# Swapping the two operands of the output products, with the result turned on VectorE

## The chip, the cores and the metric

The kernel runs on one core of a Trainium2 chip. The metric is the device time of one execution in microseconds (us). The kernel before took 787.72 us in the median of three runs (786.14 to 789.25).

Engines: TensorE (PE, its weight loads PEld) multiplies a stationary operand of up to 128x128 with a moving operand and adds into banks of PSUM; VectorE (DVE) and ScalarE (ACT) work elementwise over 128 partitions; SyncE (SP) here only issues DMAs.

## The reference

Attention over 4 batches, 8 heads, 576 positions and 64 columns a head (half the heads see a local window of 32, half see every 32nd position), then two layers on the 2304 tokens x 512 columns that come out:

```python
def _moe_ref(x, w1, w2, w3, w_out):          # d_model 512, d_ff 1024
    a = x @ w1
    b = x @ w2
    h = a * b @ w3
    return h @ w_out

def _moe2_ref(x, w_in, w_out):               # d_model 512, d_ff 2048
    h = x @ w_in
    g = h * (1.0 / (1.0 + np.exp(-1.702 * h)))
    return g @ w_out
```

All values are float32. The change concerns the last product only, g @ w_out with g of 2304x2048 and w_out of 2048x512.

## The kernel before

A float32 product is made of three products of a shorter type. Each operand is split in a high part (a ScalarE copy, line 168) and a low part (the difference, VectorE, line 174), and TensorE adds hi x lo, lo x hi and hi x hi; `ORDER` lists these pairs.

The last layer is stage 4, from 427.5 us to the end. It goes over three blocks of 768 tokens, each block in two halves of `HT` = 384 tokens, and uses a scheme with seven products instead of eight for a 2x2 split of tokens and columns. A block has two phases:

- Eight *quads* (class `Quad`). A quad makes seven products of x with w_in (`product`, line 1233, six matmuls of 128x384 each), puts gelu on them and keeps five combinations in a `part` tile. Between its products stand pieces of the second product for the quad before.
- The *sweep* (`after`): five factors of w_out times eight chunks, 40 pieces and one left over from the last quad.

A *piece* (line 1244) is one product of a chunk of g, 128 features by 384 tokens, with 256 columns of a w_out factor. Before the change g's chunk is stationary, one of its three tiles of 128 tokens at a time, and the factor's 256 columns move: 3 token tiles x 3 pairs = nine matmuls of 128x256. The sums stand in PSUM with tokens on the partitions, in two banks: `acc[0]` has token tiles 0 and 1 (512 columns), `acc[1]` has tile 2 (256). There are 56 pieces a block, 15 in quads and 41 in the sweep, 168 in all.

Each sweep piece needs a fresh split of its chunk: a `sp` tile, seven of them, high part on ScalarE, low part on VectorE.

Six results (`Out`: c11, u1, z1, c22, c21, c12) leave PSUM in a block, as copies on ScalarE or additions on VectorE into `ob` tiles (three buffers). Four of them, c11, c22, c21 and c12, are output and go out with `put`, one DMA of 384 KB on SP each; c12 of the last block goes out in two.

SP also loads the w_out factors (line 1172, from `tdram` into a ring of eight slots of two pieces each) and the split w_in chunks of the quads to come (line 1078, `fetched`, 896 KB); such a chunk is split in turn into `hl` tiles (one ScalarE operation, two on VectorE).

The order of all this is written out as a list of times: `D(t, f, ...)` puts step f at time t, with `MM` and `PC` the assumed costs of a product and a piece. The list is sorted and emitted once; each engine then takes its own instructions in that order and waits where an operand is not there.

Of the kernel before, what the change touches and what calls it, by code (L numbers as in the profile page):

```python
# [11 lines left out]
F32 = mybir.dt.float32  # L12
# [5 lines left out]
AF = mybir.ActivationFunctionType  # L18
ALU = mybir.AluOpType
PSUM = bass.MemoryType.PSUM  # L20

P = 128
B, H, S, D = 4, 8, 576, 64
# [17 lines left out]
ORDER = ((0, 1), (1, 0), (0, 0))  # L41
BT = 768
HT = BT // 2
NB = NT // BT
NU = 8
# [82 lines left out]

def wout_units(w):

    q = w.reshape(2, NU, P, 2, 256)
    return np.stack([q[0, :, :, 1], q[0, :, :, 0], q[1, :, :, 0], q[1, :, :, 1]], axis=2)


# [1 line left out]
def body(ctx: ExitStack, tc, ql, vl, qs, vs, qmask, w1, w2, w3t, wo, win, wout, out):  # L136
    nc = tc.nc

    def pool(name, bufs=1, stack=ctx, **kw):
        return stack.enter_context(tc.tile_pool(name=name, bufs=bufs, reuse_waits="tile", **kw))  # L140
# [91 lines left out]
    def turn(k):  # L232
        turns[k] = turns.get(k, 0) + 1
        return turns[k] % 2
# [6 lines left out]
    def room(what, n, w, tag, bufs):  # L241
        if what + str(n) in lent:
            return lent[what + str(n)]
        return aq.tile([P, w], F32, tag=tag, name=tag, bufs=1 if few else bufs)

    def load_qk(n):
        if n in qraw:
            return
        b, kind, c = PIECES[n]
        if kind == "l":  # L250
            t = room("q", n, NQL, "ql", 2)
            load(t, ql[b * NB3 + c], NQL)
        else:
            t = room("q", n, NQS, "qs", 2)
            load(t, qs[b * 2 + c], NQS)
        qraw[n] = t
# [199 lines left out]
    for i in (0, 2):  # L456
        t = xas.tile([P, KC * S], F32, tag="hl"[i // 2], name="lent")
# [3 lines left out]
    wide = {}  # L461
# [38 lines left out]
    acc = {}  # L500
# [17 lines left out]
    def half_step(k, i, h):  # L518
# [11 lines left out]
            x, x, 3, BODY, op0=ALU.logical_shift_left, op1=ALU.bitwise_and  # L530
# [236 lines left out]
    def back_parts(m):  # L767

        st = {}

        def load_():
            st[0] = p1.tile([P, HB], F32, tag="abf", name="abf", bufs=4)
            nc.sync.dma_start(st[0], abdram[0, m])

        def hi():
            hold[0, m] = abs_[m // 4][:, m % 4]
            split_hi(hold[0, m][:, 0], st[0])

        def lo():
            split_lo(hold[0, m][:, 1], st[0], hold[0, m][:, 0])  # L780

        return load_, hi, lo

    STEP = 1.7
    for sw in range(2):
        for g in range(MC):
# [3 lines left out]
            i = 14 + MC * sw + g  # L790
# [13 lines left out]
    for m in range(4):  # L804
        load_, hi, lo = back_parts(m)
# [322 lines left out]
    for u in range(1, NU):  # L1128
        at = -6.6 if u == 1 else 8 + UNIT * (u - 2)
# [4 lines left out]
    for n, (lo, hi, a, b, c) in enumerate(((4, 6, 32.1, 40.2, 41.6), (5, 7, 40.05, 46.9, 47.7))):  # L1134
        lo, hi = slot[lo][:, :7 * 256], slot[hi][:, :7 * 256]
# [12 lines left out]
    p2 = pool("p2", stack=right1, side="right")  # L1148
# [33 lines left out]
    def do(at, f, *args, **kw):  # L1182
        steps4.append((at, lambda: f(*args, **kw)))
# [10 lines left out]
    class Split:  # L1194

        def __init__(self, src, room=None):
            self.src, self.room = src, room
# [37 lines left out]
                    start=(first and kk == 0 and (a, c) == ORDER[0]), stop=(kk == 1 and (a, c) == ORDER[-1]), skip_group_check=True,  # L1235
                )

    def piece(acc, b, j, i, g, opens=False, ts=range(HT // P)):

        t3 = factor[b, j, i // 2]  # L1240
        for t in ts:
            to = acc[t // 2][:, t % 2 * 256:t % 2 * 256 + 256]
            for n, (a, c) in enumerate(ORDER):
                nc.tensor.matmul(  # L1244
                    to, g.t[:, a, t * P:(t + 1) * P], t3[:, i % 2, c], start=(opens and i == 0 and n == 0 and t % 2 == 0),
                    stop=(i == NU - 1 and n == 2), skip_group_check=True,
                )

    WIDE = (slice(0, 512), slice(512, 768))

    class Out:

        def room(self):
            self.t = p2.tile([P, HT // P, 256], F32, tag="ob", name="ob", bufs=3)
            self.o = self.t.rearrange("p t n -> p (t n)")

        def copy(self, acc, n):
            if n == 0:
                self.room()
            nc.scalar.activation(self.o[:, WIDE[n]], acc[n][:, :768 - 512 if n else 512], AF.Copy)  # L1260

        def add(self, acc, n, other):
            if n == 0 and other is not self:
                self.room()
            nc.vector.tensor_tensor(self.o[:, WIDE[n]], acc[n][:, :768 - 512 if n else 512], other.o[:, WIDE[n]], op=ALU.add)

        def put(self, b, right, d, lo=0, hi=HT // P):
            c0 = b * BT + right * HT
            nc.sync.dma_start(
                out[c0 + lo * P:c0 + hi * P, d * 256:d * 256 + 256].rearrange("(t p) n -> p t n", p=P), self.t[:, lo:hi]  # L1270
            )

    MM, PC = 1.05, 1.07
    QUAD = 7 * MM + 2 * PC
    SWEEP = ((S2, 1), (S1, 4), (S3, 3), (S4, 0), (B22, 2))
    BLOCK = NU * QUAD + PC * (2 + 5 * NU)

    class Quad:

        def __init__(self, b, i, X, Y, pre):  # L1280
# [29 lines left out]
            if pre:  # L1310
                D(4.2, piece, X, b, B11, i - 1, pre.c11, True)
            D(5.27, prod, "x", 4, 5, False, False)
            D(6.32, prod, "z", 6, 2, False)
            if pre:
                D(7.37, piece, Y, b, B21, i - 1, pre.a12, True)
# [3 lines left out]
            if i == NU - 1:  # L1319
                D(8.4, piece, X, b, B11, i, self.c11, True)  # L1320
                end += PC
# [40 lines left out]
    def after(b, q, X, Y):  # L1362
        A0 = b * BLOCK + NU * QUAD + PC
        D = lambda t, *a, **k: do(A0 + t, *a, **k)
        order = [(n, i) for n in range(5) for i in range(NU)]
        pos = [s if s < 2 else s + 1 for s in range(len(order))]
        final = b + 1 == NB
        sp = [
            Split(lambda n=n, i=i: parts[i][:, SWEEP[n][1]], yq[:, i // 2, i % 2] if final and n == 4 else None) for n, i in order
        ]  # L1370
        D(PC * 2, piece, Y, b, B21, NU - 1, q.a12, True)
        for s, (n, i) in enumerate(order):
            if final and n == 4:
                for m, ts in enumerate(((0, 1), (2,))):
                    D(PC * (33 + (0, 8 * 2 / 3)[m] + i * (2 - m) / 3) + 0.01, piece, X, b, SWEEP[n][0], i, sp[s], False, ts)
            else:
                D(PC * pos[s] + 0.01, piece, (X, Y)[n % 2], b, SWEEP[n][0], i, sp[s], n == 1)
            if i % 2:
                D(PC * (pos[s] + 1) + 0.02, t_more)
            if s < 3:  # L1380
                D(-QUAD - PC + 5.3 + 0.05 * s, sp[s].hi)
                D(-QUAD - PC + (7.0, 8.3, 8.4)[s], sp[s].lo)
            else:
                ahead = 6 if final and n == 4 else 3
                D(PC * (pos[s] - ahead) + 0.1 + 0.01 * (ahead > 3), sp[s].hi)
                D(PC * (pos[s] - ahead) + 0.65 + 0.01 * (ahead > 3), sp[s].lo)
        D(PC * 3 + 0.02, t_more, 2)
        c11, u1, z1, c22, c21, c12 = (Out() for _ in range(6))
        for n in range(2):
            D(-MM + 0.05 + 0.05 * n, c11.copy, X, n)  # L1390
            D(3.3 + 1.1 * n, c11.add, Y, n, c11)
            D(PC * 9 + 0.05 + 0.02 * n, u1.copy, X, n)
            D(PC * 17 + 0.05 + 0.02 * n, z1.copy, Y, n)
            D(PC * 25 + 0.1 + 1.07 * n, c22.add, X, n, z1)
            D(PC * 33 + 0.1 + 1.07 * n, c21.add, Y, n, u1)
            D(PC * (41 - (8 / 3 if final and n == 0 else 0)) + 0.02 + 0.01 * n, c12.copy, X, n)
        D(5.6, c11.put, b, 0, 0)
        D(PC * 25 + 2.4, c22.put, b, 1, 1)
        D(PC * 33 + 2.4, c21.put, b, 1, 0)
        if final:  # L1400
            D(PC * 41 - 2.5, c12.put, b, 0, 1, 0, 2)
            D(PC * 41 + 0.1, c12.put, b, 0, 1, 2, 3)
        else:
            D(PC * 41 + 0.1, c12.put, b, 0, 1)
        if b + 1 < NB:
            n = (b + 1) * NU
            do(A0 + 2.7, W[n].hi)
            D(5.3, W[n].lo, 0, 1024)
            D(7.0, W[n].lo, 1024, 7 * 256)
            D(-NU * QUAD + 4.5 * QUAD, y_fetch, b + 1, 0)  # L1410
            D(-PC - QUAD + 0.4, y_fetch, b + 1, 1)
            for kk, at in ((0, 8.0), (1, 17.5)):
                gaps = (0.3, 1.9, 3.0, 3.7, 4.6, 4.8, 5.8, 6.0, 7.5)
                for m, g in enumerate(gaps):
                    D(at + g, lambda m=m, kk=kk, b=b: more_steps(b, kk)[m]())
            D(27.5, W[n + 1].fetch)
            D(28.5, W[n + 2].fetch)
            D(35.0, W[n + 1].hi)
            D(38.0, W[n + 1].lo, 0, 1024)
            D(39.1, W[n + 1].lo, 1024, 7 * 256)  # L1420
# [3 lines left out]
    def more_steps(b, kk):  # L1424
        if (b, kk) not in cache:
            cache[b, kk] = y_steps(kk, dict(more))
        return cache[b, kk]
# [19 lines left out]
    for b in range(NB):  # L1447
        X, Y = [None] * 2, [None] * 2
# [6 lines left out]
        q = None  # L1455
        for i in range(NU):
            q = Quad(b, i, X, Y, q)
            n = b * NU + i
            at = b * BLOCK + i * QUAD
# [42 lines left out]
```

## Time and profile before

| | us |
|---|---|
| median of three runs | 787.72 |
| the profiled execution | 789.37 |
| its span, first to last instruction | 787.6 |
| TensorE busy | 768.0 |
| VectorE busy | 543.9 |
| ScalarE busy | 469.1 |
| matmuls of the pieces (x1440 and x72) | 179.5 and 8.8 |

Busy time of matmuls overlaps, since they are pipelined: 1440 of them count 282 ns each, while one starts about 120 ns after the other. What TensorE's work costs in time is read from the chain of waits, where a run of matmuls has a length and a count. The granted TensorE clock is 0.996 over the span.

### The profile page before, as it was taken

What the parts mean: (1) busy time and instruction counts of PE and PEld (TensorE: products, weight loads), DVE (VectorE), ACT (ScalarE), POOL (GpSimd) and SP (SyncE); (2) the same over time, 40 slices, a digit from 0 to 9 for tenths busy, and PEclk for the clock granted to TensorE, in tenths of its full rate; (3) what the DMA queues carried; (4) which work ended last, traced back from release to release, by engine and by line L of the source; (5) the groups of instructions that cost most, each with busy time, mean ns of one, the idle gap of its engine ahead of it and who ended that gap; (6) DMA issues with size and microseconds to landing.
All of it is one profiled execution on the core that took longest, in us unless ns stands there. A gap on an engine that the chain in (4) does not pass through costs nothing.

```text
span 787.6 us, 17841 instructions
## 1 busy us (share of the span) xinstructions
PE 768.0 (98%) x7259; PEld 746.4 (95%) x7259; DVE 543.9 (69%) x1044; ACT 469.1 (60%) x951; POOL 7.3 (1%) x15
## 2 busy tenths in 40 slices
PE   4899999999999999999999999999999999999998
PEld 4799999988889999999999999999999999999998
DVE  4799755588458475788775788794677794677743
ACT  5777654567466273655465766674666673666552
POOL 2000000000000000000000000000000000000000
PEclk9899999999999999999999999999999999999999
DMA  8987455632887646395998738789354489343382
GB/s 262 302 306 243 134 201 201 220 113 84 267 263 257 230 145 212 138 280 209 242 288 242 312 134 255 292 279 378 112 195 150 165 274 380 109 166 104 114 280 89
DMA packets 68641, 169.82 MB, mean 216 GB/s; under 512 B 5968, under 2 KB 39248, under 8 KB 66000
## 3 DMA queue, kind: packets, MB, share of 16 engines
q1 hardware_dynamic: 68416, 168.65, 63.8%
q8 instruction: 57, 0.93, 0.5%
q14 instruction: 24, 0.20, 0.1%
q10 hardware_dynamic: 144, 0.04, 0.0%
HBM read 132.49 MB, written 36.18 MB: 214 GB/s over the span
## 4 chain that ended last, share of the span: by engine, by line
PE 85%; DMA 7%; DVE 4%; ACT 2%; issue 1%; SPq 0%; DVEq 0%; ACTq 0%
PE acc L1244 23%; PE ps L1233 22%; PE ps L442 22%; PE ps L909 8%; PE acc L1090 3%; PE acc L755 3%; DMA raw<-in_w 2%; DMA ql<-in_ql 2%; PE pvq L395 1%; PE sc L304 1%; DMA lent<-in_qs 1%; DMA vst<-in_vs 1%; DVE w L174 1%; ACT w L168 1%; DMA abf<-abdram 1%
## 5 line engine op out<-in xcount | busy, mean ns | idle before, releaser
L1244 PE MATMUL acc<-w,sp 128*128 128x256 f32 x1440 | 179.5, 282 | 0.0
L1244 PEld LDWEIGHTS acc<-w,sp 128*128 128x128 f32 x1440 | 177.8, 191 | 0.0
L1233 PE MATMUL ps<-yq,hl 128*128 128x384 f32 x924 | 168.1, 335 | 0.0
L1233 PEld LDWEIGHTS ps<-yq,hl 128*128 128x128 f32 x924 | 158.7, 188 | 0.9 <-DVE part L1189 0.6
L174 DVE TENSOR_TENSOR sp<-part,sp 128x384 fp32r<-128x384 f32 x136 | 71.5, 553 | 60.2 <-ACT sp L168 60.2
L442 PE MATMUL ps<-xbh,w 128*128 128x288 f32 x512 | 102.6, 295 | 0.3 <-DVE w L174 0.2
L442 PE MATMUL ps<-xah,w 128*128 128x288 f32 x512 | 102.1, 294 | 0.0
L909 PE MATMUL ps<-ab,w 128*128 128x288 f32 x576 | 81.3, 298 | 1.4 <-ACT ysb L917 1.4
L442 PEld LDWEIGHTS ps<-xbh,w 128*128 128x128 f32 x512 | 81.9, 188 | 0.8 <-DVE w L174 0.7
L442 PEld LDWEIGHTS ps<-xah,w 128*128 128x128 f32 x512 | 82.0, 188 | 0.0
L909 PEld LDWEIGHTS ps<-ab,w 128*128 128x128 f32 x576 | 77.2, 188 | 3.0 <-ACT ysb L917 1.9
L442 PE MATMUL ps<-xbl,w 128*128 128x288 f32 x256 | 77.1, 301 | 0.0
L442 PE MATMUL ps<-xal,w 128*128 128x288 f32 x256 | 76.3, 298 | 0.0
L1186 ACT ACTIVATE part<-part 128x384 f32<-128x384 f32 x72 | 37.9, 526 | 61.6 <-DVE part L1189 61.6
L168 ACT ACTIVATE sp<-part 128x384 fp32r<-128x384 f32 x136 | 64.0, 518 | 11.1 <-PE acc L1244 10.2
L442 PEld LDWEIGHTS ps<-xbl,w 128*128 128x128 f32 x256 | 48.0, 188 | 0.8
L442 PEld LDWEIGHTS ps<-xal,w 128*128 128x128 f32 x256 | 48.0, 188 | 0.4
L174 DVE TENSOR_TENSOR ab<-abf,ab 128x288 fp32r<-128x288 f32 x64 | 28.4, 454 | 26.2 <-ACT ab L168 26.2
L755 PE MATMUL acc<-w,w 128*128 128x512 f32 x192 | 44.2, 391 | 0.1
L755 PEld LDWEIGHTS acc<-w,w 128*128 128x128 f32 x192 | 35.8, 188 | 8.2 <-DVE w L174 0.5
L174 DVE TENSOR_TENSOR hl<-fetched,hl 128x1024 fp32r<-128x1024 f32 (+1 forms) x40 | 43.3, 1083 | 0.0
L168 ACT ACTIVATE ab<-abf 128x288 fp32r<-128x288 f32 x64 | 27.2, 441 | 24.7 <-DVE abf L973 21.7
(193 smaller groups left out, 1048.8 us busy)
## 6 DMA issues: line engine op xcount, KB each, us to landing
w<-tdram SPq DMA_DIRECT2D x84, 512.0 KB, 4.7
fetched<-widram SPq DMA_DIRECT2D x20, 896.0 KB, 6.8
raw<-in_win SPq DMA_DIRECT2D x8, 1024.0 KB, 6.2
widram<-x SPq DMA_DIRECT2D x8, 896.0 KB, 7.1
raw<-in_wout SPq DMA_DIRECT2D x7, 1024.0 KB, 7.2
tdram<-raw SPq DMA_DIRECT2D x6, 896.0 KB, 5.8
tdram<-sums SPq DMA_DIRECT2D x6, 896.0 KB, 9.1
raw<-in_w3t SPq DMA_DIRECT2D x10, 512.0 KB, 4.9
```

Of the source, the lines that this page charges most:

```text
L168: nc.scalar.activation(hi, src, AF.Copy)
L174: e.tensor_tensor(lo, src, r(hi), op=ALU.subtract)
L304: nc.tensor.matmul(sc[32 * h:32 * h + 32, u, NJ * r:NJ * r + NJ], t[rows, at_:at_ + 32], t[rows, QW + QPAD + at_:QW + QPAD + at_ + NJ], st ...
L395: nc.tensor.matmul(pv[rows, h // 2, :, i], v[:, i, h], ps[:, i, h], start=True, stop=True)
L442: nc.tensor.matmul(ps, ws[a][m // 2][:, at:at + P], xh[c][:, k, cols], start=(k == 0 and (a, c) == ORDER[0]), stop=(k == KC - 1 and (a, c) ...
L755: nc.tensor.matmul(acc[f], hl[:, a, f * P:(f + 1) * P], wor[c][g], start=(g == 0 and (a, c) == ORDER[0]), stop=(g == MC - 1 and (a, c) == ...
L909: nc.tensor.matmul(yacc[n], wfs[a][k][:, n * P:(n + 1) * P], hold[s % 2, k][:, c], start=(k == 0 and (a, c) == ORDER[0]), stop=(k == MC - ...
L1090: nc.tensor.matmul(st[0], wfs[a][k][:, n * P:(n + 1) * P], hold[hb, k][:, c], start=(k == 0 and (a, c) == ORDER[0]), stop=(k == MC - 1 and ...
L1186: nc.scalar.activation(out(), src(), func)
L1233: nc.tensor.matmul(ps, w[a][:, f * 256 + kk * P:f * 256 + (kk + 1) * P], yq[:, b, kk, c], start=(first and kk == 0 and (a, c) == ORDER[0]) ...
L1244: nc.tensor.matmul(to, g.t[:, a, t * P:(t + 1) * P], t3[:, i % 2, c], start=(opens and i == 0 and n == 0 and t % 2 == 0), stop=(i == NU - ...
```

## The change

The two operands exchange sides. A w_out factor's 128 columns become the stationary operand and g's 384 tokens move: 2 column halves x 3 pairs = six matmuls of 128x384 a piece. The sums stand transposed in PSUM: output columns on the partitions, tokens along the bank, `acc[n]` with 384 tokens of column half n.

To store rows of tokens again, VectorE turns the result in blocks of 32x32 (`turn`, from an `ob` tile into an `ot` tile of 192 tokens; `turn_one` for the last output, straight from PSUM). A block of 32 columns and 32 tokens is turned within its 32 partitions, so the columns that end up side by side come from four groups of 32 partitions: `wout_units` reorders w_out's columns so that each group holds 64 neighbouring output columns. `put` writes one group per DMA, four for each `ot` tile. In all 26 transposes are added, and 13 stores become 104. `ob` has two buffers instead of three and `ot` three. `PC` goes from 1.07 to 1.04. In the last block the last eight pieces go by column halves instead of token tiles.

```diff
 def wout_units(w):
-    q = w.reshape(2, NU, P, 2, 256)
+    q = w.reshape(2, NU, P, 2, 4, 2, 32).transpose(0, 1, 2, 3, 5, 4, 6).reshape(2, NU, P, 2, 256)
...
-    def piece(acc, b, j, i, g, opens=False, ts=range(HT // P)):
+    def piece(acc, b, j, i, g, opens=False, ns=range(2)):
         t3 = factor[b, j, i // 2]
-        for t in ts:
-            to = acc[t // 2][:, t % 2 * 256:t % 2 * 256 + 256]
-            for n, (a, c) in enumerate(ORDER):
+        for n in ns:
+            for m, (a, c) in enumerate(ORDER):
                 nc.tensor.matmul(
-                    to, g.t[:, a, t * P:(t + 1) * P], t3[:, i % 2, c], start=(opens and i == 0 and n == 0 and t % 2 == 0),
-                    stop=(i == NU - 1 and n == 2), skip_group_check=True,
+                    acc[n][:, :HT], t3[:, i % 2, c, n * P:(n + 1) * P], g.t[:, a], start=(opens and i == 0 and m == 0),
+                    stop=(i == NU - 1 and m == 2), skip_group_check=True,
                 )
...
+        def turn(self, h):
+            self.T[h] = p2.tile([P, TB, 2, 32], F32, tag="ot", name="ot", bufs=3)
+            nc.vector.transpose(
+                self.T[h].rearrange("p b n i -> p n b i"),
+                self.t[:, :, h * 32 * TB:(h + 1) * 32 * TB].rearrange("p n (b i) -> p n b i", i=32),
             )
+        def turn_one(self, acc, n, h):
+            if h == 0:
+                self.T[n] = p2.tile([P, 2, TB, 32], F32, tag="ot", name="ot", bufs=3)
+            nc.vector.transpose(
+                self.T[n][:, h], acc[n][:, h * 32 * TB:(h + 1) * 32 * TB].rearrange("p (b i) -> p b i", i=32)
+            )
+        def put(self, b, right, d, h, n=None):
+            t, lo, wide = (self.T[h].rearrange("p b n i -> p b (n i)"), 0, 64) if n is None else (self.T[n][:, h], 32 * n, 32)
+            c0 = b * BT + right * HT + h * 32 * TB
+            to = out[c0:c0 + 32 * TB, d * 256:d * 256 + 256].rearrange("(b j) (a x) -> a j b x", j=32, a=4)
+            for a in range(4):
+                nc.sync.dma_start(to[a, :, :, lo:lo + wide], t[32 * a:32 * a + 32])
-    MM, PC = 1.05, 1.07
+    MM, PC = 1.05, 1.04
...
+                D(PC * 41 + 1.2 + 0.7 * n, c12.turn, n)
+                D(PC * 41 + 1.9 + 0.7 * n, c12.put, b, 0, 1, n)
+        for h in range(2):
+            for o, at, to in ((c11, 5.2, (0, 0)), (c22, PC * 25 + 2.3, (1, 1)), (c21, PC * 33 + 2.3, (1, 0))):
+                D(at + 0.7 * h, o.turn, h)
+                D(at + 0.7 * h + 0.7, o.put, b, *to, h)
```

The order of instructions, first VectorE's at the end of the first block, before the change. `sp` and `hl` are the low parts of the chunks, `ob<-acc,ob` the second addition of c21, and the last row is the first addition of the next block. What stands in brackets are the counters that a row waits for; DMAHW0 to DMAHW7 count landings of DMAs that SP issued.

```order
L1265 TENSOR_TENSOR ob<-acc,ob 128x256 [waits PE_49]
L174 TENSOR_TENSOR sp<-part_5831,sp 128x384 [waits Activation_49]
L174 TENSOR_TENSOR hl<-fetched,hl 128x1024 [waits DMAHW0_49]
L174 TENSOR_TENSOR sp<-part_5832,sp 128x384 [waits Activation_49]
L174 TENSOR_TENSOR hl<-fetched,hl 128x768
L174 TENSOR_TENSOR sp<-part_5833,sp 128x384 [waits Activation_49]
L174 TENSOR_TENSOR sp<-part_5834,sp 128x384 [waits Activation_49]
L1189 TENSOR_TENSOR part_5654<-ps,s_7004 128x384 [waits PE_49,Activation_49]
```

The same place after the change: two turns of c21 and two of c12.

```order
L1265 TENSOR_TENSOR ob<-acc,ob 128x384 [waits PE_49]
L174 TENSOR_TENSOR sp<-part_5825,sp 128x384 [waits Activation_49]
L1269 STREAM_TRANSPOSE ot<-ob 128x2x6x32 [waits DMAHW3_49,DMAHW2_49,DMAHW4_49,DMAHW1_49,DVE_49]
L174 TENSOR_TENSOR sp<-part_5826,sp 128x384 [waits Activation_49]
L1269 STREAM_TRANSPOSE ot<-ob 128x2x6x32 [waits DMAHW4_49,DMAHW5_49,DMAHW3_49,DMAHW2_49]
L174 TENSOR_TENSOR hl<-fetched,hl 128x1024 [waits DMAHW7_49]
L174 TENSOR_TENSOR sp<-part_5827,sp 128x384 [waits Activation_49]
L174 TENSOR_TENSOR hl<-fetched,hl 128x768
L174 TENSOR_TENSOR sp<-part_5828,sp 128x384 [waits Activation_49]
L1269 STREAM_TRANSPOSE ot<-ob 128x2x6x32 [waits DMAHW6_49,DMAHW1_49,DMAHW7_49,DMAHW0_49,Activation_49]
L1269 STREAM_TRANSPOSE ot<-ob 128x2x6x32 [waits DMAHW6_49,DMAHW1_49,DMAHW7_49,DMAHW0_49,DVE_49]
L1189 TENSOR_TENSOR part_5654<-ps,s_6866 128x384 [waits PE_49,Activation_49]
```

Each turn has a place of its own between two low parts, and waits for the landing of the four stores that read its `ot` buffer last.

SP's queue in the same sweep, from the two fetches on, before the change:

```order
L1078 DMA fetched<-widram 128x1792 [waits DMAHW0_49,DVE_49,Activation_49]
L1078 DMA fetched<-widram 128x1792 [waits DMAHW1_49,DVE_49,Activation_49]
L1172 DMA w_1624<-tdram 128x1024 [waits DMAHW2_49,PE_49]
L1269 DMA out<-ob 128x3x256 [waits DMAHW3_49,DVE_49]
L1172 DMA w_1624<-tdram 128x1024 [waits DMAHW4_49,PE_49]
L1172 DMA w_1625<-tdram 128x1024 [waits DMAHW5_49,PE_49]
```

And after it, where c22's store has become eight:

```order
L1078 DMA fetched<-widram 128x1792 [waits DMAHW7_49,DVE_49]
L1172 DMA w_1624<-tdram 128x1024 [waits DMAHW0_49,PE_49]
L1078 DMA fetched<-widram 128x1792 [waits DMAHW1_49,DVE_49,Activation_49]
L1286 DMA out<-ot 32x6x64 [waits DMAHW2_49,DVE_49]
L1286 DMA out<-ot 32x6x64 [waits DMAHW3_49]
L1286 DMA out<-ot 32x6x64 [waits DMAHW4_49]
L1286 DMA out<-ot 32x6x64 [waits DMAHW5_49]
L1286 DMA out<-ot 32x6x64 [waits DMAHW6_49,DVE_49]
L1286 DMA out<-ot 32x6x64 [waits DMAHW7_49]
L1286 DMA out<-ot 32x6x64 [waits DMAHW0_49]
L1286 DMA out<-ot 32x6x64 [waits DMAHW1_49]
L1172 DMA w_1624<-tdram 128x1024 [waits DMAHW2_49,PE_49]
```

The counters go round by eights, one step for each DMA.

## Rows read from the trace of the kernel before

**Rows 1.** The page: engine shares (busy us, share, instructions) and the chain that ended last.

```profile
PE 768.0 (98%) x7259; PEld 746.4 (95%) x7259; DVE 543.9 (69%) x1044; ACT 469.1 (60%) x951; POOL 7.3 (1%) x15
...
PE 85%; DMA 7%; DVE 4%; ACT 2%; issue 1%; SPq 0%; DVEq 0%; ACTq 0%
```

**Rows 2.** Chain of waits in order of time: start us, length us, what.

```profile
502.37 44.27 PE acc L1244 x369
```

**Rows 3.** Chain of waits, 477 to 483 us.

```profile
477.17 1.07 PE acc L1244 x9
478.24 2.08 PE ps L1233 x12
```

**Rows 4.** Groups by line and shape, VectorE: busy us, mean ns | idle before.

```profile
L174 DVE TENSOR_TENSOR sp<-part,sp 128x384 fp32r<-128x384 f32 x136 | 71.5, 553 | 60.2 <-ACT sp L168 60.2
...
L1189 DVE TENSOR_TENSOR part<-part 128x768 f32<-128x768 f32 x24 | 22.9, 953 | 1.8 <-ACT part L1186 1.8
...
L529 DVE TENSOR_SCALAR xw<-xw 128x512 int32<-128x512 int32 x20 | 8.4, 422 | 3.4 <-ACT xw L527 3.4
```

**Rows 5.** Timeline of the end: start us, length us, engine, instruction [idle before].

```profile
782.78 1.60 PE L1244 MATMUL acc<-w,yq 128*128 128x256 f32 x12
...
784.41 0.38 ACT L1260 ACTIVATE ob<-acc 128x256 f32<-128x256 f32 x1 [2.28 <-PE acc L1244]
784.82 0.34 SPq L1269 DMA_DIRECT2D out<-ob  x1
```

**Rows 6.** The tile `ob`: the stores (issue in ns, min/median/max) and their landing.

```profile
L1269 SPq DMA_DIRECT2D out<-ob x13: 344/389/1422, 508.2 to 784.8; - x13
...
DMA to landing us min/median/max: 1.7/6.2/10.9
```

**Rows 7.** Timeline of SP, 175 to 182 us.

```profile
177.43 1.85 SPq L773 DMA_DIRECT2D abf<-abdram  x4
```

**Rows 8.** Timeline of SP, 527 to 552 us.

```profile
529.82 1.22 SPq L1078 DMA_DIRECT2D fetched<-widram  x2
531.55 0.32 SPq L1172 DMA_DIRECT2D w<-tdram  x1
531.96 1.42 SPq L1269 DMA_DIRECT2D out<-ob  x1
533.71 6.80 SPq L1172 DMA_DIRECT2D w<-tdram  x4
540.60 0.39 SPq L1269 DMA_DIRECT2D out<-ob  x1
542.35 4.64 SPq L1172 DMA_DIRECT2D w<-tdram  x3
547.22 0.55 SPq L1269 DMA_DIRECT2D out<-ob  x1
```

**Rows 9.** Windows: length; PE, PEld, DVE, ACT, POOL busy; clock, DMA share, GB/s.

```profile
530.00:548.00 18.00, 18.00 (x148) 18.00 (x147) 9.78 (x19) 7.03 (x13) 0.00 (x0) 1.00 0.98 360
785.60:786.20 0.60, 0.00 (x0) 0.00 (x0) 0.00 (x0) 0.00 (x0) 0.00 (x0) 1.00 0.65 219
```

**Rows 10.** Timeline of ScalarE, 536 to 553 us.

```profile
537.51 1.70 ACT L168 ACTIVATE hl<-fetched 128x1792 fp32r<-128x1792 f32 x1 [3.27 <-DMA fetched<-widram]
...
549.42 0.53 ACT L1186 ACTIVATE part<-part 128x384 f32<-128x384 f32 x1 [1.21 <-DVE part L1189]
549.85 0.47 ACT L1298 ACTIVATE u<-ps 128x384 f32<-128x384 f32 x1
```

**Rows 11.** Waits of SP's queue: what for, us in total, times, longest.

```profile
SPq L1172 <- PE acc L1244: 172.6, 68, 14.4
```

**Rows 12.** Timeline of VectorE, 536 to 553 us.

```profile
548.83 0.56 DVE L1189 TENSOR_TENSOR part<-ps,s 128x384 f32<-128x384 f32 x1 [4.41 <-PE ps L1233]
```

**Rows 13.** Chain of waits, 544 to 560 us.

```profile
546.64 11.70 PE ps L1233 x66
```

More of the change, by code (lines that the diff above doesn't have):

```diff
@@ L1247, in piece, with __init__ @@
                 )
-    WIDE = (slice(0, 512), slice(512, 768))
+    TB = HT // 64
     class Out:
-        def room(self):
-            self.t = p2.tile([P, HT // P, 256], F32, tag="ob", name="ob", bufs=3)
-            self.o = self.t.rearrange("p t n -> p (t n)")
+        def __init__(self):
+            self.T = {}
         def copy(self, acc, n):
             if n == 0:
-                self.room()
-            nc.scalar.activation(self.o[:, WIDE[n]], acc[n][:, :768 - 512 if n else 512], AF.Copy)
+                self.t = p2.tile([P, 2, HT], F32, tag="ob", name="ob", bufs=2)
+            nc.scalar.activation(self.t[:, n], acc[n][:, :HT], AF.Copy)
@@ L1262, in add @@
         def add(self, acc, n, other):
[L1263 to L1270, printed above, removed]
-            )
@@ L1273, in body @@
-    MM, PC = 1.05, 1.07
+            self.t = other.t
+            nc.vector.tensor_tensor(self.t[:, n], acc[n][:, :HT], other.t[:, n], op=ALU.add)
+        def turn(self, h):
[3 more added lines that the diff above has]
+                self.t[:, :, h * 32 * TB:(h + 1) * 32 * TB].rearrange("p n (b i) -> p n b i", i=32),
+            )
+        def turn_one(self, acc, n, h):
[4 more added lines that the diff above has]
+            )
@@ L1373, in after @@
             if final and n == 4:
-                for m, ts in enumerate(((0, 1), (2,))):
-                    D(PC * (33 + (0, 8 * 2 / 3)[m] + i * (2 - m) / 3) + 0.01, piece, X, b, SWEEP[n][0], i, sp[s], False, ts)
+                for m in range(2):
+                    D(PC * (33 + 4 * m + i / 2) + 0.01, piece, X, b, SWEEP[n][0], i, sp[s], False, (m,))
             else:
@@ L1395, in after @@
             D(PC * 33 + 0.1 + 1.07 * n, c21.add, Y, n, u1)
[L1396 to L1404, printed above, removed]
+            if final:
+                for h in range(2):
+                    D(PC * (37 + 4 * n) + 0.1 + 0.1 * h, c12.turn_one, X, n, h)
+                    D(PC * (37 + 4 * n) + 0.11 + 0.1 * h, c12.put, b, 0, 1, h, n)
+            else:
+                D(PC * 41 + 0.02 + 0.01 * n, c12.copy, X, n)
+                D(PC * 41 + 1.2 + 0.7 * n, c12.turn, n)
+                D(PC * 41 + 1.9 + 0.7 * n, c12.put, b, 0, 1, n)
+        for h in range(2):
+            for o, at, to in ((c11, 5.2, (0, 0)), (c22, PC * 25 + 2.3, (1, 1)), (c21, PC * 33 + 2.3, (1, 0))):
+                D(at + 0.7 * h, o.turn, h)
+                D(at + 0.7 * h + 0.7, o.put, b, *to, h)
         if b + 1 < NB:
```

## The prediction

> **What bounds the kernel now.** I read the page's shares first: TensorE is busy 98% of the span, VectorE 69%, and 85% of the chain that ended last is TensorE's [rows 1]. Then the chain of waits in order of time, over the last 360 us, the stage that the change touches: it consists of TensorE pieces that join end to end. Each block's sweep is one unbroken run of 369 matmuls of 256 columns in 44.27 us, 120.0 ns each [rows 2]. Between the quads the same matmul takes 1.07/9 = 118.9 ns, and one of 384 columns 2.08/12 = 173.3 ns [rows 3]. So a column costs 0.465 ns in a short matmul and 0.451 ns in a long one, and work on the other engines is free as long as it comes before TensorE asks for its result. Last, the timelines of the queues and of VectorE where a block ends, and the end of the kernel: only there does TensorE lean on something else.
>
> **TensorE.** There are 168 pieces, 123 in sweeps and 45 between quads. A piece goes from nine matmuls of 256 columns to six of 384, which is the same number of columns. In a sweep that is 1.080 - 6 x 0.1733 = 1.040, so 0.040 us less; elsewhere 1.070 - 1.040 = 0.030. Sum: 123 x 0.040 + 45 x 0.030 = 6.3 us. If the sweep keeps half of what its matmuls take above those between quads, (1.080 - 1.070) x 123 / 2 = 0.6 us comes off; I take 6.2, bounds 5.6 to 6.3. All of it is on the path.
>
> The Trainium skill (TensorE: Matmul & The Clock Gate, section Back-to-back issue gap) gives an isolated gap of N / 2.4 + 2.5 ns for N columns. By that, an estimate, nine at 109.2 against six at 162.5 ns save 1.3 us in all. Rows 3 show 118.9 and 173.3 instead, and the sum goes by them.
>
> **VectorE.** 26 transposes are new, 22 of 384 elements a partition and four of 192. No transpose is in the trace. The nearest groups are a two-operand operation of 128x384 at 553 ns, below it one of 128x512 with a single operand at 422, above it one of 128x768 at 953 [rows 4]. I take 0.55 and 0.35 us: 22 x 0.55 + 4 x 0.35 = 13.5 us, in a stretch of 360 us in which VectorE has room. The output copies and additions keep their size (2 x 384 for 512 + 256). Beside TensorE this costs nothing, unless a transpose stands in front of something that is late already. There are two such places.
>
> **The end of the kernel.** Now the last matmul ends at 784.38, a ScalarE copy of 0.38 us follows, and one store is issued at 784.82 [rows 5]. It lands 1.7 us later, the shortest of the 13 [rows 6], and the span ends at 787.6. Afterwards each output is eight DMAs on SP, the last one sixteen. An issue there takes 344 ns at least and 389 in the median [rows 6], and four in a row go at 1.85/4 = 0.46 us [rows 7]; I take 0.42. Call the end of the last matmul T. The eight stores of c21 can start when its second addition and first turn are done, about T - 6.2. Sixteen issues (c21, and c12's first half) then last until T + 0.5, and the last eight until T + 3.9. The last lands at T + 3.9 - 0.4 + 1.7 = T + 5.2, where it is now T + 2.2. So the end gives back 3.0 us; with 0.344 us an issue it is 2.3, at most (0.46) 4.5.
>
> **Where a block ends** (547 and 666 us). Every DMA on SP carries a wait for one of eight landing counters in turn, so it waits until the eighth DMA before it has landed. Before, 13 DMAs between 529.8 and 547.2 are two fetches, three stores and eight loads [rows 8], and the queues are 98% busy there [rows 9]. The first fetch lands just before 537.5, when ScalarE takes it [rows 10], 7.7 us after its issue, and the second should by that land near 540. Afterwards the eight stores of c22 stand behind these fetches: the last two must wait for their landings. The factor loads behind them come up to 7 us later. That costs nothing, since SP has waited for TensorE to free their slots (172.6 us over the span) [rows 11], and each is used at least 14 pieces later. But the stores of c21, behind four of those loads, go out at about 540 + 0.4 + 4 x 0.4 = 542 at the earliest and 543.3 by the landings that the loads wait for; I take 543.
>
> That matters because `ot` has three buffers. c12's second turn needs the buffer of c21's first half, thus the landing of its four stores: 543 + 6.2 (median) = 549.2. Behind that turn, on VectorE, stands the addition with which the next block opens. It began at 548.83 after idling 4.41 us for TensorE [rows 12]; then ScalarE's gelu and the copy of u, from 549.42 to 550.32 [rows 10]. TensorE's fifth product adds to the bank that this copy reads, and is due at 546.64 + 4 x 1.04 = 550.8 [rows 13]. So there is 0.5 us of slack now and no waiting. After the change the sweep's end comes 41 x 0.04 = 1.65 earlier, and c21's stores 30 x 0.04 = 1.2 earlier. The copy then ends at 548.0 + 0.55 + 0.56 + 0.53 + 0.47 = 550.1, against a due time of 549.15: about 1.0 us lost. The landing that the turn waits for is the lever. With 1.7 us (the shortest) nothing is lost, with 10.9 (the longest) [rows 6] 5.7. As the packets also get smaller I take 1.2 us, twice: 2.4.
>
> **Packets.** A store of 384 KB goes from rows of 1024 bytes to 1536 rows of 256, the last output's to 128. In the last store 128 packets of 1024 bytes kept 16 engines 65% busy for 0.6 us [rows 9], 49 ns each. If a packet's price goes with its bytes, nothing is added; if every packet costs 49 ns, a store costs 1536 x 49 / 16 = 4.7 us of all engines instead of 1.2. I take some 20 ns, between them: 1.9 us a store, hidden except in the landing times above. The Trainium skill (DMA: Bandwidth & Descriptors, section Specifications) asks for at least 512 bytes for full rate and says that below this the engine reads, modifies and writes. All new stores are below; no row of before shows such a store of this size, and the rule would push towards the dear end, the second rival.
>
> **Sum:** -6.2 + 3.0 + 2.4 = -0.8 us. The profiled run took 789.4 (its span of 787.6 and 1.8 around it), which makes 788.6 on its own scale; the median of the three runs stands 1.7 below it, at 787.7, and I forecast 787.0 against that. Own range: with end 2.3 and block ends 0.8 each it is 785.4; with 5.6 saved, 4.5 and 2 x 2 it is 790.6.
>
> **Rivals.**
> Nothing is lost at the block ends. SP's stores land before VectorE gets to the last turn, as half of the 13 landings took less than 6.2 us, down to 1.7. Then -6.2 + 3.0 = -3.2: 784.5. Against it stands the 98% of the queues in just that stretch.
>
> Slower: dear small packets. c21's first four stores land 10.9 us after their issue rather than 6.2, since the stores of c22 ahead of them and their own take up to 3.5 us more each of saturated queues. That gives 1.2 + 4.7 = 5.9 us at each block end, and the end at its upper bound: -6.2 + 11.8 + 4.5 = +10.1, 797.8; halfway, 793. It decides as soon as these stores take 2.4 us longer than the median, from 8.6 us on: 2 x 3.6 + 3.0 - 6.2 = +4. For it: the largest of the present landings is from a full queue. Against: the stores carry as many bytes as before, and the stretch before and behind is at a lower load (98% is that of 18 us).
>
> The gain is not there: what six matmuls cost is set by the new roles of the operands (weights now come from the ring of factors), or 1.3 us is all. Then -1.3 + 3.0 + 2.4 = +4.1: 791.8. Against: the products at 173.3 ns are of just this form, 128x384 moving with a fresh load for each.
>
> **Chances.** Forecast 0.49, nothing lost at block ends 0.23, dear packets 0.24, no gain 0.04. A measurement of this kernel tells a change from none at about 0.5%, 3.9 us: below 783.8 is faster, above 791.7 slower. A third of the first rival and a little of the forecast lie below: 0.14. Slower: most of dear packets, half of no gain, and a tail of the forecast's block ends: 0.29. The rest, 0.57. The range for 8 in 10 reaches from 783.3 (block ends free, so -6.3 + 2.3 = -4.0, and half a per mille for the measurement) to 796 (most of the way to dear packets); the forecast's own is 785.4 to 790.6.
>
> **What will show it.** The chain's sweep pieces at 41 x 1.04 = 42.6 us, and the matmul groups with 1008 matmuls of 128x384 at L1243. The transposes near 0.55 us. SP issuing stores without a pause at the end, and some 5 us between the last matmul and the last landing. At each block end an idle time of VectorE before a transpose, released by a DMA from `ot`, and TensorE idle for 1 to 2 us about four products later. Wrong if TensorE waits inside a sweep (a turn ahead of a late split), if SP's loads of factors come too late for it, or if a store lands after more than 8.6 us.

## The result and the profile after

The changed kernel takes 793.85 us in the median of 8 runs (791.12 to 796.95), the kernel before 787.67 in 8 (786.14 to 791.42). The ratio is 1.0064, 95% interval 1.0045 to 1.0082: slower by some 5 us by the ratio and 6 by the medians. Timed a second time it was 794.74 against 788.14, ratio 1.0079 (1.0052 to 1.0106). The forecast of 787.0, a hair faster, was wrong, though 793.85 lies in its range, near its slow end.

The profiled execution took 791.34 us, near the fastest of the eight. It has a span of 789.5 us, only 1.9 over that of before. It entered the last stage 1.7 us earlier, though, at 425.68 where before began at 427.35; the stages ahead are the same code in both and move by this much from one execution to the next (this stage starts between 424.1 and 427.4 in the traces of all the runs here). From there to the end it is 363.9 us against 360.2, and so 3.6 longer.

First the page of the kernel after, its engine shares:

```profile
PE 763.1 (97%) x6755; PEld 740.8 (94%) x6755; DVE 554.8 (70%) x1070; ACT 469.1 (59%) x949; POOL 7.4 (1%) x15
```

Against [rows 1] TensorE has 4.9 us less to do and VectorE 10.9 more. Next the chain of waits of the last stage, in order of time (start us, length us, what):

```profile
500.22 28.09 PE acc L1243 x162
528.34 0.42 ACT sp L168
528.75 9.17 DMA fetched<-widram
537.94 1.69 DMA out<-ot
...
541.84 5.45 DMA out<-ot
547.52 0.44 issue
547.97 0.53 DVE part L1189
548.52 0.52 ACT part L1186
549.04 0.39 ACT u L1313
549.48 9.14 PE ps L1233 x42
...
662.42 5.00 DMA out<-ot
...
669.55 7.55 PE ps L1233 x42
...
739.51 42.66 PE acc L1243 x246
```

The last line answers to [rows 2]: the sweep of the last block takes 42.66 us where it took 44.27, just what six matmuls for nine should bring. But where [rows 13] had products joining on without a break, the chain now leaves TensorE. It runs through the landing of a store from `ot`, the turn (under "issue"), VectorE's addition, gelu, the copy of u, and only then back. The waits in that stretch, 540 to 552 us (who waited, for whom, us in total, times, longest):

```profile
DVE ot L1269 <- DMA out<-ot: 2.9, 1, 2.9
...
PE ps L1233 <- ACT u L1313: 1.9, 1, 1.9
...
PEld acc L1243 <- DVE sp L174: 0.6, 2, 0.3
```

And VectorE's timeline at the end of the first block (start us, length us, instruction, idle before and what ended it):

```profile
538.75 0.58 DVE L1269 STREAM_TRANSPOSE ot<-ob 128x384 f32<-128x384 f32 x1 [0.64 <-DMA out<-ot]
539.25 1.18 DVE L174 TENSOR_TENSOR hl<-fetched,hl 128x1024 fp32r<-128x1024 f32 x1
540.36 0.55 DVE L174 TENSOR_TENSOR sp<-part,sp 128x384 fp32r<-128x384 f32 x1
...
544.00 0.58 DVE L1269 STREAM_TRANSPOSE ot<-ob 128x384 f32<-128x384 f32 x1 [1.76 <-ACT ob L1261]
547.47 0.58 DVE L1269 STREAM_TRANSPOSE ot<-ob 128x384 f32<-128x384 f32 x1 [2.89 <-DMA out<-ot]
547.97 0.52 DVE L1189 TENSOR_TENSOR part<-ps,s 128x384 f32<-128x384 f32 x1
```

The turn at 547.47 waits for the stores of c21's first half, and right behind it stands the addition that [rows 12] shows at 548.83 with nothing to wait for but TensorE. The turn at 538.75 waits too, for stores of c22; the two rows behind it are late for that, and the `sp` split at 540.36 comes too late for the sweep (the 0.6 us of weight loads above).

The second block end has a like idle time, 1.7 us at 669. One thing differs: behind the first, 42 products take 9.14 us, behind the second 7.55. The windows show why (length; PE, PEld, DVE, ACT, POOL busy; granted clock; DMA share; GB/s):

```profile
547.50:549.50 2.00, 0.12 (x2) 0.03 (x1) 0.99 (x2) 0.98 (x3) 0.00 (x0) 1.00 0.53 102
549.50:551.50 2.00, 2.00 (x7) 2.00 (x8) 0.56 (x1) 0.71 (x2) 0.00 (x0) 0.55 1.00 379
551.50:553.50 2.00, 2.00 (x9) 2.00 (x8) 0.63 (x2) 0.52 (x1) 0.00 (x0) 0.59 0.99 305
553.50:558.00 4.50, 4.50 (x28) 4.50 (x27) 3.50 (x6) 2.21 (x5) 0.00 (x0) 1.00 0.78 190
```

Column seven: after the idle time TensorE ran at 0.55 and 0.59 in the mean of these windows, that is mostly at 1.2 GHz instead of 2.4, and took 7 and 9 matmuls in 2 us where 11 or 12 fit. That is another 1.6 us lost.

Last the end, from the timeline of all engines and the tile `ot`:

```profile
767.50 20.08 SPq L1286 DMA_DIRECT2D out<-ot  x32
...
773.66 8.48 PE L1243 MATMUL acc<-yq,w 128*128 128x384 f32 x48
...
782.19 0.65 DVE L1277 STREAM_TRANSPOSE ot<-acc 128x192 f32<-128x192 f32 x2 [3.52 <-PE acc L1243]
```

```profile
L1286 SPq DMA_DIRECT2D out<-ot x104: 315/439/1955, 506.2 to 787.1; - x104
L1269 DVE STREAM_TRANSPOSE ot<-ob x22: 535/573/586, 505.6 to 775.7; 128x384 f32<-128x384 f32 x22
L1277 DVE STREAM_TRANSPOSE ot<-acc x4: 340/362/383, 778.0 to 782.5; 128x192 f32<-128x192 f32 x4
...
DMA to landing us min/median/max: 1.5/3.5/8.1
```

The last matmul ends at 782.14, the last store is issued at 787.1, 5.0 later, and the span ends 7.4 behind the matmul; in [rows 5] these were 0.4 and 3.2.

### The profile page after: what moved, and what is told of

It is laid out like the page before. It is cut to its first block, busy times and chain, and to the rows that moved or that the text cites. A ratio compares the mean times of both kernels' runs of the same rounds, so it can differ in the third digit from the quotient of the medians.

```text
span 789.5 us, 16971 instructions
## 1 busy us (share of the span) xinstructions
PE 763.1 (97%) x6755; PEld 740.8 (94%) x6755; DVE 554.8 (70%) x1070; ACT 469.1 (59%) x949; POOL 7.4 (1%) x15
## 4 chain that ended last, share of the span: by engine, by line
PE 84%; DMA 6%; DVE 3%; ACT 3%; issue 2%; SPq 1%; DVEq 0%; ACTq 0%
PE ps L442 26%; PE ps L1233 21%; PE acc L1243 18%; PE ps L909 8%; PE acc L1090 3%; PE acc L755 3%; DMA out<-ot 2%; DMA fetched<-widram 1%; PE sc L304 1%; PE pvq L395 1%; DMA lent<-in_qs 1%; PE sc L294 1%; DMA abf<-abdram 1%; SPq L1286 1%; DMA lent<-in_ql 1%
## 5 line engine op out<-in xcount | busy, mean ns | idle before, releaser
L1243 PE MATMUL acc<-sp,w 128*128 128x384 f32 x960 | 174.2, 334 | 0.0
L1243 PEld LDWEIGHTS acc<-sp,w 128*128 128x128 f32 x960 | 167.0, 188 | 0.6 <-DVE sp L174 0.6
L1233 PEld LDWEIGHTS ps<-yq,hl 128*128 128x128 f32 x924 | 162.2, 189 | 4.6 <-ACT u L1313 4.3
```

Source lines behind the costliest of these rows:

```text
L1233: nc.tensor.matmul(ps, w[a][:, f * 256 + kk * P:f * 256 + (kk + 1) * P], yq[:, b, kk, c], start=(first and kk == 0 and (a, c) == ORDER[0]) ...
L1243: nc.tensor.matmul(acc[n][:, :HT], t3[:, i % 2, c, n * P:(n + 1) * P], g.t[:, a], start=(opens and i == 0 and m == 0), stop=(i == NU - 1 a ...
```

## The experiments

Theory: the price is three waits of known place: VectorE's turns for `ot` buffers at the block ends (with the clock behind them), the same within the sweeps, and SP's issuing at the end. Rival: stores in small rows are dear by themselves, wherever they are. Each experiment was timed beside the kernel before; us are medians.

**The changed kernel again**, for the spread of its waits. No edit.

> The changed kernel once more, beside the others of this call. The theory: VectorE's last turn at a block end waits for the landing of the stores that still read its buffer, so TensorE idles about 2 us at 543 to 550 and at 663 to 670; and where the granted clock falls after such an idle time, as it did behind the first (0.55 to 0.59 for some 4 us, 320 ns a matmul in place of 173), 1.7 us more go. So both idle times are there again, at 1.5 to 2.5 us, and behind them the clock may fall at none, one or both. Time 793 to 795, some 6 above the kernel before. The rival, that small stores are dear all over the stage: the idle times would differ from one execution to the next with the DMA load, and the products between blocks would start late in other places too.

Measured 794.74. Idle times again, 5.2 us in both together and 2.7 in the longer, and the clock down behind the first only: 42 products in 9.12 and in 7.55 us. Within the sweeps the late splits cost more than the first time (1.4 us of weight loads waiting for `sp`, four times). The last stage takes 366.1 us in this trace, 5.9 more than before, where the first profile had 3.6 more.

**c21's first turn into another buffer.** The tile `a12` is idle in a sweep and has the same size.

```diff
-        def turn(self, h):
-            self.T[h] = p2.tile([P, TB, 2, 32], F32, tag="ot", name="ot", bufs=3)
+        def turn(self, h, lent=False):
+            if lent:
+                self.T[h] = f32("a12").rearrange("p (b n i) -> p b n i", n=2, i=32)
+            else:
+                self.T[h] = p2.tile([P, TB, 2, 32], F32, tag="ot", name="ot", bufs=3)
...
-                D(at + 0.7 * h, o.turn, h)
+                D(at + 0.7 * h, o.turn, h, o is c21 and h == 0)
```

> The turn of c21's first half goes into the tile of a12, which is idle in a sweep, in place of the ring of three; all else stays, the 104 stores, their order and their size too. So c12's second turn no longer needs c21's landing. Theory: the two idle times at the block ends go (2.05 and 1.88 us), and with them the clock's fall (1.7 us where it came): 4 to 7 us less than the changed kernel, about 787 to 789. The end still costs 4 us more than before. Rival (small stores are dear, SP is held up): c12's turns or the next factors wait for something else in the same place, and the time stays within 1.5 us of the changed kernel, 792 to 795.

Measured 786.06 against 788.14, ratio 0.9979 (0.9967 to 0.9992): one buffer turns the change from slower to slightly faster, by 8.7 us in the medians against the changed kernel timed with it, 7.9 by the ratios (4.7 between the nearest ends of their intervals). That is more than the 4 to 7 expected, though not clear of it. In the trace the waits within the sweeps went too, which the 4 to 7 did not count: c21's second turn no longer needs c22's landing. Its chain of waits has no DMA from the first sweep to the last:

```profile
499.85 42.64 PE acc L1243 x246
542.49 11.71 PE ps L1233 x66
...
616.61 42.64 PE acc L1243 x246
659.25 11.69 PE ps L1233 x66
...
733.33 42.66 PE acc L1243 x246
```

SP's queue was held up as in the changed kernel, and TensorE never waited for it (its timeline: start us, length us, what):

```profile
529.60 8.56 SPq L1289 DMA_DIRECT2D out<-ot  x8
538.25 1.82 SPq L1172 DMA_DIRECT2D w<-tdram  x4
540.16 1.97 SPq L1289 DMA_DIRECT2D out<-a  x4
542.23 4.49 SPq L1289 DMA_DIRECT2D out<-ot  x4
```

Stores, rows and queues are the same as in the changed kernel; so small stores are not dear by themselves, wherever they are. Whether it is their small rows that make them land late, as the prediction's "dear packets" has it, this run cannot tell; the small stores in the kernel before, below, can. The end costs what it did (the span ends 7.5 us behind the last matmul), and with that the sum closes: -6.2 + 4.3 = -1.9, where the last stage takes 358.2 us in the trace against 360.2 before.

**Two buffers in place of three**, the suspected wait made longer: `bufs=3` of both `ot` tiles becomes `bufs=2`.

> The changed kernel with two ot buffers in place of three, nothing else: the suspected wait made longer. Theory: c12's first turn now needs c21's first half landed, and the second turn its second half, which landed 1.5 us later; so TensorE's idle time at both block ends grows from 1.9 to 3.0 us as seen so far to 3.4 to 4.5. If an idle time of that length brings the granted clock down, it now falls behind the second as it did behind the first, for 3 to 4 us (1.7 us lost each). 797 to 799. Rival (the stores themselves are the price, buffers don't matter): 793 to 795, as with three.

Measured 797.91, ratio 1.0120 (1.0078 to 1.0163). The time is as expected, but the interval overlaps that of three buffers (1.0052 to 1.0106), so it is the trace that shows the difference. The idle times are not as expected: 3.1 and 2.4 us, hardly more than with three. What grew is the wait within the sweeps, as c21's turns now both wait for c22's stores. These are TensorE's waits over the stage; the second row, its weight loads waiting for `sp`, stood at 0.6 to 1.9 in the three profiles with three buffers:

```profile
PE ps L1233 <- ACT u L1313: 5.5, 2, 3.1
PEld acc L1243 <- DVE sp L174: 4.2, 6, 1.1
```

The clock fell behind both idle times here, the second, shorter one included (TensorE's timeline: start us, length us, what, idle before):

```profile
673.25 9.12 PE L1233 MATMUL ps<-yq,hl 128*128 128x384 f32 x42 [2.37 <-ACT u L1313]
```

**The changed kernel a third time**, one run.

> The changed kernel once more, for its profile: idle times of 1.9 to 3.0 us at 548 and 669, the clock down behind the first (as in both profiles so far) and not behind the second. Should it be down behind the second and not the first, it is chance which of them it meets.

791.79 us. Idle 2.7 and 2.5 us, and no fall at all: 42 products in 7.55 and 7.58. So it isn't the place.

```profile
549.84 7.55 PE L1233 MATMUL ps<-yq,hl 128*128 128x384 f32 x42 [2.75 <-ACT u L1313]
```

**The pieces without the turns**, with `ob` back at three buffers. It leaves out the turns and so stores the output in another order.

```diff
-                self.t = p2.tile([P, 2, HT], F32, tag="ob", name="ob", bufs=2)
+                self.t = p2.tile([P, 2, HT], F32, tag="ob", name="ob", bufs=3)
...
+            nc.sync.dma_start(
+                out[c0:c0 + HT, d * 256 + lo:d * 256 + lo + wide].rearrange("(t p) x -> p t x", p=P),
+                t.rearrange("p (t x) -> p t x", t=3),
             )
...
-            for a in range(4):
-                nc.sync.dma_start(to[a, :, :, lo:lo + wide], t[32 * a:32 * a + 32])
```

> The pieces as in the changed kernel, but nothing is turned: the transposed sums go out as they lie in ob (three buffers), one store of 384 KB in rows of 1024 bytes for each output, the last in two of rows of 512; so the output is in another order than the reference's. It measures what the six matmuls of 384 columns save by themselves. Theory: sweeps of 42.6 us and no idle time at the block ends; 6.2 us less than the kernel before, 781 to 782.5. Rival (the gain is not there, or is lost within the sweeps): 785 to 788.

Measured 781.61, ratio 0.9919 (0.9900 to 0.9937): 6.5 us less, as much as the matmuls were to save. Its sweeps are 42.64, 42.64 and 42.66 us.

**Small stores alone**, in the kernel before.

```diff
-            nc.sync.dma_start(
-                out[c0 + lo * P:c0 + hi * P, d * 256:d * 256 + 256].rearrange("(t p) n -> p t n", p=P), self.t[:, lo:hi]
-            )
+            for a in range(4):
+                nc.sync.dma_start(
+                    out[c0 + lo * P:c0 + hi * P, d * 256 + a * 64:d * 256 + a * 64 + 64].rearrange("(t p) n -> p t n", p=P),
+                    self.t[:, lo:hi, a * 64:a * 64 + 64],
+                )
```

> The kernel before with its old pieces and no turn, but each store split in four of 64 columns, so rows of 256 bytes in place of 1024 and 52 stores in place of 13. Theory (the bytes set the queues' time, and SP only matters at the end): no idle time at the block ends; at the end c12's first part is out of the way, and the last four stores issue from 0.43 to 1.9 us behind the last matmul, so the last landing is 1.4 us later than now: 788.9 to 789.5. Rival (small rows are dear): TensorE waits at block ends for ob buffers or late factors, 791 or more, and a single store of 32 KB takes over 3 us to land at the end, where the queues are empty.

Measured 789.68 against 787.83, ratio 1.0017 (1.0001 to 1.0033), within the theory's 788.9 to 789.5 by the ratio (789.2). No block end shows an idle TensorE, and the stores land in 1.5 us at best, 5.2 in the median, where 384 KB in one took 1.7 and 6.2 [rows 6]:

```profile
DMA to landing us min/median/max: 1.5/5.2/9.9
```

What it lost is at its end: the span ends 4.7 us behind the last matmul (781.84), where it was 3.2. Small rows are not free, though. Behind other transfers, a store of 384 KB in rows of 1024 bytes lands 1.0 us after the transfer ahead of it in the kernel before (median); here the four parts land 0.33 us one after another, 1.3 in all, and in the changed kernel the eight parts 0.17, 1.4 in all. That is far from the 3.5 us more that "dear packets" needs.

**The end on two queues**, for the last block's c21 and c12.

```diff
-                nc.sync.dma_start(to[a, :, :, lo:lo + wide], t[32 * a:32 * a + 32])
+                queue = nc.scalar if b + 1 == NB and d != right and a % 2 else nc.sync
+                queue.dma_start(to[a, :, :, lo:lo + wide], t[32 * a:32 * a + 32])
```

> In the last block, half of the stores of c21 and c12 are issued by ScalarE, which is idle there, and half by SP. Theory: the end is bound by issuing (24 issues at 0.48 us behind one another on SP), so the last landing comes about 3 us nearer to the last matmul (from 6.6 us behind it to about 3.7), and the time is 3 us under the changed kernel, about 791. Rival (the landing of stores with rows of 128 and 256 bytes bounds the end): the last landing stays 6 us or more behind the last matmul, the time the same as the changed kernel.

Measured 791.99, 2.7 less than the changed kernel timed with it; but the ratio, 1.0052 (1.0034 to 1.0070), overlaps that one's (1.0052 to 1.0106), and the way differs from the forecast. In its profile the span ends 5.9 us behind the last matmul (785.54), where it was 7.4; by the forecast it would be 4.5 (the landing at 3.7, and the 0.8 from there to the span's end). The queues ran side by side only in part:

```profile
779.21 8.59 ACTq L1287 DMA_DIRECT2D out<-ot  x12
780.87 8.54 SPq L1287 DMA_DIRECT2D out<-ot  x13
```

SP's part began only at 780.87, 1.7 us after ScalarE's, which is what a store takes to land there. After that both issue, with pauses of up to 1.4 us on SP and 2.2 on ScalarE, and the 25 issues of the two rows take 10.2 us where 24 on SP alone took 11.8. In the order of instructions both queues draw on the same eight landing counters, and SP's last store of c22 waits for one that a store of ScalarE has to raise first. The end gave 1.5 us of the 3 forecast. What else there is in the 2.7 is not separable from the block ends, which vary from run to run, so this run bears out issuing as the bound only in part.

**A shorter end**, on top of the lent buffer: c12's column halves are turned into one tile, so that the last output needs 8 stores and not 16.

```diff
-            if h == 0:
-                self.T[n] = p2.tile([P, 2, TB, 32], F32, tag="ot", name="ot", bufs=3)
+            if n == 0:
+                self.T[h] = p2.tile([P, TB, 2, 32], F32, tag="ot", name="ot", bufs=3)
             nc.vector.transpose(
-                self.T[n][:, h], acc[n][:, h * 32 * TB:(h + 1) * 32 * TB].rearrange("p (b i) -> p b i", i=32)
+                self.T[h][:, :, n], acc[n][:, h * 32 * TB:(h + 1) * 32 * TB].rearrange("p (b i) -> p b i", i=32)
...
-                    D(PC * (37 + 4 * n) + 0.11 + 0.1 * h, c12.put, b, 0, 1, h, n)
+                    if n:
+                        D(PC * 41 + 0.11 + 0.1 * h, c12.put, b, 0, 1, h)
```

> With the lent buffer, and the last output's two column halves turned into one tile: after the last matmul two short turns, then eight stores with rows of 256 bytes in place of eight of 128 with eight more just before them. Theory (issuing on SP bounds the end): the last store is issued at 0.45 + 7 x 0.485 = 3.85 us behind the last matmul and lands 1.6 later, at 5.4 where it was 6.67; 1.2 us less than with the lent buffer alone, about 784.8. Rival (rows of 128 bytes land slowly, the number of issues matters little): landings fall by more than that, to 4 us or less; or nothing changes because SP is not what is waited for.

Measured 785.63 against 787.83, ratio 0.9971 (0.9956 to 0.9987). The end is as forecast: eight issues in 3.73 us from 0.45 behind the last matmul (776.33), and the span ends 6.3 behind it in place of 7.5:

```profile
776.37 0.65 DVE L1280 STREAM_TRANSPOSE ot<-acc 128x192 f32<-128x192 f32 x2 [3.52 <-PE acc L1243]
776.78 3.73 SPq L1289 DMA_DIRECT2D out<-ot  x8
```

The gain over the lent buffer alone is inside the intervals, so only the trace shows it.

**That end on two queues**: the queue line of "The end on two queues", with `d > right` in place of `d != right`, so c12 alone.

> As the packed end, with half of the last eight stores issued by ScalarE. No store waits any more for the landing of one that the other queue issued shortly before. Theory: four issues on each queue, the last at 0.45 + 3 x 0.485 = 1.9 us behind the last matmul, landing at 3.5; 3.1 us under the lent buffer alone, about 783.0, the fastest of all that compute the reference. Rival: the two queues issue in turn rather than side by side, or the counters hold one for the other as with the first split; then it stays at 784 to 785.

Measured 784.86, ratio 0.9966 (0.9950 to 0.9982), the lowest median of those that compute the reference; but its interval holds the packed end's, and the trace shows no gain: the span ends 6.8 us behind the last matmul (775.67), 0.5 later than with one queue. The rival was right about the mechanism: one queue is held for the other again, SP until 777.78, 1.7 us behind ScalarE's first issue:

```profile
776.12 1.83 ACTq L1290 DMA_DIRECT2D out<-ot  x4
777.78 2.57 SPq L1290 DMA_DIRECT2D out<-ot  x5
```

The first of SP's five stores is c21's last: in the order it waits for the counter of ScalarE's first store, and c12's four stand behind it.

## Why the prediction was wrong

**The matmuls: right.** 6.2 us was the forecast, sweeps of 42.64 to 42.66 us came where nothing waited (1.6 less, three times), and the run without turns shows 6.5 in all. The gap that the Trainium skill gives (TensorE: Matmul & The Clock Gate, section Back-to-back issue gap) would have made it 1.3, by the prediction's estimate; the measurement decides.

**The turns on VectorE: right in size.** 573 and 362 ns against 0.55 and 0.35.

**Small packets: right that they are not the price.** At the end, with empty queues, a store of 256-byte rows lands in 1.6 to 1.8 us, and the kernel before with such stores lost 1.3 us by its ratio, at its end. The Trainium skill (DMA: Bandwidth & Descriptors, section Specifications) asks for 512 bytes for full rate; the traces agree that there is a loss below it, and it is small: 1.3 to 1.4 us for 384 KB in rows of 256 bytes against 1.0 in rows of 1024, where I had taken 1.9 against 1.2.

**The block ends: the step that failed.** The place, the cause and the chain behind it were as written. The term was not: 1.2 us each, where 1.7 to 2.7 of idle time came, and two costs that the sum held at nothing, the clock's fall and the waits within the sweeps.

- The landing. I took 543 + 6.2, the median landing of a 384 KB store over the whole stage. The store of c21 itself, issued at 540.60 in the kernel before, took 7.9:

```profile
out<-ob SPq DMA_DIRECT2D x1, 384.0 KB, 7.9
```

  After the change the stores went out from 540.27, but behind four factor loads of 512 KB issued at 538.4 to 539.8, and they land after those:

```profile
w<-tdram SPq DMA_DIRECT2D x4, 512.0 KB, 5.0
out<-ot SPq DMA_DIRECT2D x8, 48.0 KB, 5.3
```

  These are the DMAs of 538 to 546 us. A store of 48 KB took 5.3 us in the median, about as long as those loads, and 1.6 to 1.8 at the kernel's end, where the queues were empty. Here the landing is set by what the queue holds, not by the store. The four stores of c21's first half are also issued one after the other, and from the first issue to the last landing, at 547.3, it is 7.0 us. Counted from the sweep's start the landing came 47.1 us behind it, where the sum had 45.6. TensorE was 0.6 us later than forecast itself, by the waits in the sweep; what is left, 0.9, is what the idle time of 1.9 has over the 1.0 that the sum worked out.
- The clock. The granted clock fell behind some of the idle times, which cost 1.6 us each time (9.14 - 7.55). It fell behind one of the two idle times in the first profile of the changed kernel, one in the second and none in the third. I had priced an idle time by its length alone.
- The sweeps. That a turn stands ahead of a late split was under "Wrong if" and had no term. c21's turn waited for c22's landing, and the weight loads behind it waited 0.6 us in one profile, 1.4 in the next and 1.9 in the third.

**The end: right in kind, short in size.** 24 issues in a row were the forecast, at 0.42 us each. They came at 0.44 plus 0.05 between them; the last was issued 5.0 us behind the last matmul, not 3.5. That makes 4.2 us by the spans' ends (7.4 - 3.2) where the sum had 3.0. It is the smaller part of the miss.

With the measured sizes the sum for the first profile is -6.2 + 3.6 (idle) + 1.6 (clock) + 0.6 (sweeps) + 4.2 (end) = +3.8, against 3.6 by the traces; for the second -6.2 + 5.2 + 1.6 + 1.4 + 4.2 = +6.2, against 5.9 by its trace; for the third -6.2 + 5.2 + 0 + 1.9 + 4.2 = +5.1, against 5.0. That the median lay within the range was luck: the range reached so far for the sake of "dear packets", and that rival gave nearly the right time for a wrong reason. Its size was reached by idle times up to twice as long as forecast, the clock and the sweeps.

## What to carry to other kernels

A result that leaves through a small ring of buffers ties the engine that fills the ring to the landing of the store; look at what stands behind that engine's instruction in order, and take the landing from the bytes ahead in the queue, not from a median. Where a buffer of the same size is idle in that phase, lend it: here nothing in the trace waited for the lent tile, and it was worth some 8 us, more than the 6.2 that the change saves on TensorE. Splitting one store in eight is paid where no work follows: count issues on the queue at the kernel's end.

## What was not expected of the hardware

The granted clock does not fall behind each idle time of TensorE. Over five profiles with ten idle times of 1.7 to 3.1 us it fell behind five, and neither length nor place tells which: 2.4 us at 671 in the run with two buffers was followed by 1.2 GHz, and 2.7 at 547 in the changed kernel's third profile was not. What decides it is open. Each fall lasted some 3.4 us and cost 1.6.

A second queue gave less than its issues suggest: with the landing counters shared, SP stood 1.7 us for ScalarE's first store. A division of the stores that avoids this was not tried.
